# A small GpSimd copy per unit in a fused attention and bilinear kernel

## The chip, the cores and the metric

The kernel runs on one core of one Trainium2 chip. The metric is the device time of one launch in microseconds (us). Times shown for a kernel are the median of its runs.

## The reference

```
scores = (q @ k^T) / 8                           per head; 4 batches, 12 heads, 448 tokens, width 64
scores = einsum('bhij,hg->bgij', scores, w_pre)  mix the heads
attn   = exp(scores - max) / (sum + 1e-9)
attn   = einsum('bhij,hg->bgij', attn, w_post)   mix the heads again
x      = (attn @ v), laid out as 1792 x 768
out    = ((x @ w_a) * (x @ w_b)) @ w_out         768 -> 1536 -> 768
```

## The kernel before

The first 480 us or so are attention, the rest is the bilinear part. The change touches attention alone.

**Units and steps.** The queries of a batch are cut into chunks of 120, 120, 120 and 88 rows, and a chunk into units of 20 (the last of a batch has 8). That makes 16 chunks and 92 units, 23 to a batch. The main loop (L565) runs over steps `s`; step `s` handles unit `s`, and below a step is named by that number, so batch 1 is steps 23 to 45.

**What a step does, in program order.** It gathers the scores of unit `s + 3` (L584), mixes the heads of unit `s` with `w_pre` (`premix`, L590), copies out the second mix of unit `s - 2`, takes maximum and exponential of unit `s` (`smax`, L596), runs the step's share of the products q by k for a later chunk (`qk`) and of attention by v (`av`), turns the row sums of unit `s` into scaled mixing weights `kr` (`norm`, L601), and mixes unit `s - 1` with `w_post` (`postmix`, L604). At the end stand the loads and copies listed in `after` for the step (L605).

**The scores' way.** `qk` writes two heads of a chunk to PSUM; ScalarE copies them to the chunk's tile `s` (L219). There are two such tiles, so chunk `c` writes where chunk `c - 2` stood. A gather is a DMA from SBUF to SBUF on SyncE's queue (SP), four for a unit of 20 rows (L235): it brings the 12 heads of 5 rows onto 60 partitions. So the first copy L219 of a chunk waits until the last gather of the chunk two before has landed. The 88-row chunk of a batch begins its `qk` at the tenth step of the batch (9, 32, 55, 78), and the last unit that reads the tile it overwrites is gathered one step before. The first chunk of the next batch begins at steps 15, 38 and 61, with two heads' products in that step.

**What GpSimd (POOL) issues, in one queue.** `load_v` (L183) loads a sixth of the next batch's v in each of steps 9 to 14 of a batch (batch 0's own v in steps 2 and 4). `load_k` (L187) stands three steps ahead of the `qk` that uses it, which comes to steps 12, 12, 13, 14, 15 and 16 of a batch; `load_q` (L194) four steps ahead, twice a chunk; `spread_q` (L203, L208) is a GpSimd copy that reorders q, one step ahead. The order of the queue is the program's order, but nothing ties it to the step: an entry starts when the one before has been issued and its own buffer is free and data there. Buffers: 10 for k, 3 for raw q, 4 for q, 2 for each half of v.

**Row sums.** `smax` has ScalarE write the row sums `rs` of a block of 10 rows (L265); `norm` has VectorE add 1e-9 to them in place (L272), take the reciprocal (L274) and scale `kf` by it to `kr` (L276). A unit has two blocks; `rs` has 4 buffers.

Of the kernel before, what the change touches and what calls it, by code (L numbers as in the profile page):

```python
# [7 lines left out]
F32 = mybir.dt.float32  # L8
# [13 lines left out]
def talking_heads_bilinear_kernel(  # L22
# [11 lines left out]
    nc = tc.nc  # L34
# [15 lines left out]
    AH = 3  # L50
# [25 lines left out]
    units = []  # L76
# [3 lines left out]
    NU = len(units)  # L80
# [9 lines left out]
    const = ctx.enter_context(tc.tile_pool(name="const", bufs=1))  # L90
# [3 lines left out]
    w_p = ctx.enter_context(tc.tile_pool(name="w", bufs=2))  # L94
# [16 lines left out]

    def ps_t():
        return ps.tile([128, 2, 512], F32, tag="t", name="pst", bufs=1)[:, 0]

    todo_at, now = {}, [0]

# [104 lines left out]
    def halves(n):  # L221
        return [(o, min(QH, n - o)) for o in range(0, n, QH)]

    def gather(u):
        c, o, n = units[u]
        sbt[u] = [sb_p.tile([128, S], F32, tag=f"sb{e}", name="sb") for e in range(2)]
        for i, (t, m) in enumerate(halves(n)):
            r = 64 * (i // 2)
            nb = chunks[c][2] // QB
            k_ = (o + t) // QB  # L230
            if k_ < nb:
                rows = st[c][:nb * QB].rearrange("(i k) h s -> k i h s", k=nb)[k_, t % QB:t % QB + m]
            else:
                rows = st[c][o + t:o + t + m]
            nc.sync.dma_start(out=sbt[u][i % 2][r:r + m * H], in_=rows)  # L235
# [21 lines left out]
    def smax(k_):  # L257
        u, j, n = k_
        m = rows_of(n)
        mp = mt.pop((u, j))  # L260
        nm = w_p.tile([128, 1], F32, tag="nm", name="nm", bufs=4)
        rs = w_p.tile([128, 1], F32, tag="rs", name="rs", bufs=4)
        a = w_p.tile([128, S], F32, tag="an", name="a", bufs=AB)
        nc.vector.tensor_reduce(nm[:m], mp[:m], axis=AXX, op=ALU.max, negate=True)  # L264
        nc.scalar.activation(a[:m], mp[:m], ACTF.Exp, bias=nm[:m], scale=1.0, accum_out=rs[:m])  # L265
        at[u, j] = (a, rs)

    def norm(k_):
        u, j, n = k_
        m = rows_of(n)  # L270
        a, rs = at.pop((u, j))
        nc.vector.tensor_scalar(rs[:m], rs[:m], 1e-9, None, op0=ALU.add)  # L272
        rc = w_p.tile([128, 1], F32, tag="rc", name="rc", bufs=4)
        nc.vector.reciprocal(rc[:m], rs[:m])  # L274
        kr = w_p.tile([128, H, QB], F32, tag="kr", name="kr", bufs=5)
        nc.vector.tensor_scalar(kr[:m], kf[:m], rc[:m], None, op0=ALU.mult)  # L276
        ant[u, j] = a, kr
# [45 lines left out]
    items, after, ready = {}, {}, {}  # L323
# [31 lines left out]
    def load_x(b, parts=(0, 1, 2)):  # L355
        if b not in xt:
            xt[b] = big.tile([128, 2, KD, S], F32R, tag="s" if b < 2 else "pt", name="xhl")
        for i in parts:
            nc.sync.dma_start(out=xt[b].bitcast(F32)[:, 1, 2 * i:2 * i + 2], in_=xd[b][:, 2 * i:2 * i + 2])
# [176 lines left out]
    with tc.manual_schedule():  # L536
        setup()
        load_q(0, 0)
        load_k(0, 0)
        load_k(0, 1)  # L540
        load_q(0, 1)
        load_k(0, 2)
        load_k(0, 3)
        act_table()
        warm_up(WARM)
        setup_mask()
        spread_q(0, 0, nc.vector)
        for i in range(G):
            if i == 1:
                spread_q(0, 1, nc.vector)  # L550
            if i + 4 < G:
                load_k(0, i + 4)
            if i == 2:
                load_q(1, 0)
                load_q(1, 1)
            qk(0, i)
        spread_q(1, 0)
        setup_w()
        nxt_g = AH + 1
        for u in range(nxt_g):  # L560
            gather(u)
        warm_up(WARM3)
        tail = iter(())

        for s in range(NU + 2):  # L565
            now[0] = s
            if s == last_prep + 1:
                open_moe()
                load_raw(order[0])
                later(lambda: load_raw(order[1]), 1)  # L570
                for i in range(3):
                    later(lambda i=i: load_x(0, (i,)), 2 + i)
                tail = tail_ops()
            if s == NU - 2:
                load_x(1)
            if s == NU - 1:
                load_x(2)
            if s in (2, 4):
                for i in range(3):
                    load_v(0, 3 * (s // 2 - 1) + i)  # L580
            b, i = divmod(s, NUB)
            if b + 1 < B and 0 <= i - V_AT < 6:
                load_v(b + 1, i - V_AT)
            while nxt_g <= min(s + AH, NU - 1) and ready.get(units[nxt_g][0], -1) < s:  # L584
                gather(nxt_g)
                nxt_g += 1
            for fn in todo_at.pop(s, ()):
                fn()
            if s < NU:
                premix(s)  # L590
            if s >= 2:
                for k_ in blocks_of(s - 2):
                    evac_p(k_)
            if s < NU:
                for k_ in blocks_of(s):
                    smax(k_)  # L596
            for it in items.get(s, ()):
                it[0](*it[1:])
            if s < NU:
                for k_ in blocks_of(s):  # L600
                    norm(k_)  # L601
            if 0 <= s - 1 < NU:
                for k_ in blocks_of(s - 1):
                    postmix(k_)  # L604
            for it in after.get(s, ()):  # L605
                it[0](*it[1:])
            if s >= last_prep + 2:
                take(tail, RATE if s < NU - LATE else RATE2)
            if s == NU:
                for _ in tail:  # L610
                    pass
                tail = split_ops(1)
                for k_ in blocks_of(NU - 1):
                    evac_p(k_)
                run_a(0, 0)
            if s == NU + 1:
                run_b(0, 0)
        for p in range(6):
            av(NA - 1, p)
        for t in sorted(todo_at):  # L620
            for fn in todo_at[t]:
                fn()
        todo_at.clear()
        load_x(3)
        for _ in tail:
            pass
        now[0] = 999
        late = conv_ops(range(2, 4))
        take(late, T1)
        run_a(0, 1)  # L630
        take(split_ops(2), 12)
        run_b(0, 1)
        take(late, T2)
        run_a(0, 2)
        take(late, T3)
        run_b(0, 2)
        for _ in late:
            pass
        run_a(1, 0)
        take(split_ops(3), 12)  # L640
        run_b(1, 0)
        todo = {(0, 3): order[4], (1, 1): order[5], (1, 2): order[6], (1, 3): order[7]}
        for i, u in enumerate(order[8:]):
            todo[2 + i // 3, i % 3 if u[0] == "f" else 2] = u
        nxt = 6
        pairs = [(0, 3), (1, 1), (1, 2), (1, 3)] + [(f, b) for f in range(2, KF) for b in range(B)]
        for i, (f, b) in enumerate(pairs):
            now[0] = 1000 + i
            for fn in todo_at.pop(now[0], ()):
                fn()  # L650
            if (f, b) in todo:
                ops, fin = conv(todo[f, b])
                for fn in ops:
                    fn()
                if nxt < len(order):
                    load_raw(order[nxt])
                    nxt += 1
            run_a(f, b)
            if (f, b) in todo:
                fin()  # L660
            run_b(f, b)
            if f == KF - 1 and b == 1:
                load_o(0)
                load_h(0)
                load_o(1)
                split_o(0)
            if f == KF - 1 and b > 1:
                for i in range(KF // 2 * (b - 2), KF // 2 * (b - 1)):
                    split_h(0, i)
            if b == B - 1:  # L670
                del wt["f", f]
        now[0] += 1
        for t in sorted(todo_at):
            for fn in todo_at[t]:
                fn()
        todo_at.clear()
        for j in range(B * KD):
            b, m = divmod(j, KD)
            load_o(j + 2)
            if m == 0 and b + 1 < B:  # L680
                load_h(b + 1)
            if j + 1 < B * KD:
                split_o(j + 1)
            if b + 1 < B and m >= 2:
                for f in range(3 * (m - 2), 3 * (m - 1)):
                    split_h(b + 1, f)
            run_o(j)
# [48 lines left out]
```

## Time and profile before

| | us |
|---|---|
| median of 3 runs | 1020.28 |
| the three runs | 1009.82, 1020.28, 1021.34 |
| the profiled execution | 1023.44 |
| its span, first to last instruction | 1021.7 |
| TensorE busy in the span | 977.9 |

Engines are named PE (TensorE matmul), DVE (VectorE), ACT (ScalarE), POOL (GpSimd) and SP (SyncE). A row of a timeline gives start, length, engine, line, operation, what it writes and reads, how many such instructions in a row, and in brackets how long the engine was idle before and what ended that. A row of stretches gives from and to, the length, then busy us and number of instructions of PE, PEld (weight loads), DVE, ACT and POOL, then the mean granted TensorE clock as a share of the full one, the mean busy share of the DMA engines, and GB/s. A row of the waits gives who waited for whom, the total in us, how often and the longest.

### The profile page before, as it was taken

The numbers are of one execution on the slowest core, as the hardware profiler recorded it, in microseconds if no ns is written. First come the engines' busy times: TensorE is split into PE (matmuls) and PEld (weight loads), VectorE is DVE, ScalarE is ACT, GpSimd is POOL, SyncE is SP. The second block draws the span as 40 slices with busy tenths as digits, with TensorE's granted clock in tenths as the row PEclk, the third lists the DMA queues.
The fourth block names the chain that finished last, engine by engine and source line by source line (L and its number), as shares of the span: only waits on it lengthen the run. The fifth ranks groups of instructions, "written<-read, shape, count | busy, mean of one in ns | idle before, by whom it ended". The sixth has DMA issues, their size and how long they took to land.

```text
span 1021.7 us, 16847 instructions
## 1 busy us (share of the span) xinstructions
PE 977.9 (96%) x6388; PEld 777.9 (76%) x6388; DVE 504.8 (49%) x1090; ACT 418.6 (41%) x854; POOL 275.2 (27%) x229
## 2 busy tenths in 40 slices
PE   7799999899999999988999999999999999999998
PEld 4356566556656566666889999999999998999997
DVE  1355445344554445567667565666555364341500
ACT  2576667466656667655321111111111143443421
POOL 4301103110121100002134323332323234554642
PEclk7999999899998999998999999999999999999999
DMA  6544336433354233347335333433323166556431
GB/s 171 158 149 149 99 121 175 151 109 108 123 173 143 87 126 108 107 153 254 111 99 190 133 115 136 144 116 118 142 108 144 74 244 235 208 181 229 157 122 67
DMA packets 63471, 146.59 MB, mean 143 GB/s; under 512 B 6252, under 2 KB 48000, under 8 KB 62368
## 3 DMA queue, kind: packets, MB, share of 16 engines
q1 hardware_dynamic: 58528, 131.11, 37.3%
q0 software_dynamic: 4864, 14.42, 5.1%
q8 instruction: 51, 0.84, 0.3%
q14 instruction: 28, 0.23, 0.1%
HBM read 80.23 MB, written 26.74 MB: 105 GB/s over the span
## 4 chain that ended last, share of the span: by engine, by line
PE 83%; DMA 9%; DVE 3%; ACT 2%; SPq 1%; issue 1%; POOL 0%; ACTq 0%; DVEq 0%
PE pp L286 13%; PE pst L218 8%; PE mp L255 7%; PE xp L311 7%; PE po L435 6%; PE po L436 6%; PE po L434 6%; DMA sb<-s 6%; PE pa L434 5%; PE pa L436 5%; PE pa L435 5%; PE pb L436 5%; PE pb L435 5%; PE pb L434 5%; DMA xd<-xs 3%; ACT s L219 1%
## 5 line engine op out<-in xcount | busy, mean ns | idle before, releaser
L286 PEld LDWEIGHTS pp<-kr,a 124*112 124x112 f32 (+1 forms) x1440 | 161.8, 184 | 51.2 <-issue 31.6
L264 DVE TENSOR_REDUCE nm<-mp 124x1 f32<-124x448 f32 x180 | 104.6, 620 | 160.8 <-PE mp L255 160.8
L286 PE MATMUL pp<-kr,a 124*112 124x120 f32 (+1 forms) x1440 | 179.3, 280 | 3.4 <-ACT pt L297 2.2
L265 ACT ACTIVATE a<-mp,nm 124x448 f32<-124x448 f32 x180 | 112.7, 631 | 94.7 <-DVE nm L264 91.9
L396 POOL TENSOR_TENSOR cvm<-cvm,cvr 128x768 int32<-128x768 int32 x36 | 67.0, 1862 | 281.2 <-DVE cvm L395 211.3
L218 PE MATMUL pst<-k,q 64*120 64x448 f32 (+1 forms) x384 | 102.9, 614 | 25.9 <-ACT s L219 25.8
L424 POOL TENSOR_TENSOR wl<-rawo,wh 128x768 fp32r<-128x768 f32 x48 | 93.7, 1974 | 105.3 <-ACT wh L423 105.3
L297 ACT COPY pt<-pp 112x480 f32<-112x480 f32 x180 | 97.0, 573 | 50.6 <-PE pp L286 50.3
L446 ACT COPY sa<-pa 128x448 f32<-128x448 f32 x48 | 25.6, 534 | 221.8 <-PE pa L436 213.7
L435 PE MATMUL po<-hl,wh 128*128 128x448 f32 x288 | 106.3, 369 | 0.7 <-DVE hl L471 0.7
L435 PE MATMUL pa<-xhl,wh 128*128 128x448 f32 x288 | 104.6, 363 | 1.7 <-DVE xhl L366 1.7
L434 PE MATMUL po<-hh,wh 128*128 128x448 f32 x288 | 106.2, 369 | 0.0
L436 PE MATMUL po<-hh,wl 128*128 128x448 f32 x288 | 106.2, 369 | 0.0
L255 PE MATMUL mp<-sb,wp 60*64 60x448 f32 x720 | 99.3, 567 | 6.7 <-ACT a L265 4.0
L434 PE MATMUL pa<-xhl,wh 128*128 128x448 f32 x288 | 104.6, 363 | 0.0
L436 PE MATMUL pa<-xhl,wl 128*128 128x448 f32 x288 | 104.4, 363 | 0.0
L219 ACT COPY s<-pst 120x896 f32<-120x896 f32 (+1 forms) x96 | 86.5, 901 | 40.2 <-PE pst L218 21.0
L436 PE MATMUL pb<-xhl,wl 128*128 128x448 f32 x282 | 102.3, 363 | 0.6 <-POOL wl L424 0.6
L434 PE MATMUL pb<-xhl,wh 128*128 128x448 f32 x282 | 102.2, 362 | 0.0
L435 PE MATMUL pb<-xhl,wh 128*128 128x448 f32 x282 | 102.2, 362 | 0.0
L218 PEld LDWEIGHTS pst<-k,q 64*120 64x120 f32 (+1 forms) x384 | 27.6, 179 | 95.7 <-ACT s L219 38.6
L471 DVE TENSOR_TENSOR hl<-hl,hh 128x448 fp32r<-128x448 f32 x48 | 57.9, 1261 | 79.4 <-ACT hh L470 79.4
(63 smaller groups left out, 1307.2 us busy)
## 6 DMA issues: line engine op xcount, KB each, us to landing
sb<-s SPq DMA_DIRECT2D x356, 105.0 KB
raw<-in_w_ab_dram SPq DMA_DIRECT2D x24, 768.0 KB
rawo<-wod SPq DMA_DIRECT2D x24, 768.0 KB
hd<-hf SPq DMA_DIRECT2D x48, 224.0 KB
raw<-in_w_out_dram SPq DMA_DIRECT2D x12, 768.0 KB
v<-in_v_dram POOLq DMA_DIRECT2D x24, 224.0 KB, 5.5
xhl<-xd SPq DMA_DIRECT2D x12, 448.0 KB
hl<-hd SPq DMA_DIRECT2D x4, 1344.0 KB
```

Source lines behind the costliest of these rows:

```text
L218: nc.tensor.matmul(sp[:n, g], lhsT=qt[c, i // QG][rows, i % QG], rhs=kt[b, i][rows])
L219: nc.scalar.copy(st[c].rearrange("p (g i) s -> p i g s", g=2)[:n, i], sp[:n])
L255: nc.tensor.matmul(mt[u, i // 2][col:col + M], lhsT=wp[r:r + m, :M], rhs=tiles[i % 2][r:r + m])
L264: nc.vector.tensor_reduce(nm[:m], mp[:m], axis=AXX, op=ALU.max, negate=True)
L265: nc.scalar.activation(a[:m], mp[:m], ACTF.Exp, bias=nm[:m], scale=1.0, accum_out=rs[:m])
L286: nc.tensor.matmul(pp[:, r, :, :n], lhsT=an[:m, r * P:(r + 1) * P], rhs=kr[:m, :, :n])
L297: nc.scalar.copy(ptt[a][:P, :, :, o:o + n], pps.pop((u, j))[:, :, :, :n])
L311: nc.tensor.matmul(xp[64 * e:64 * e + 64, p % 3, :n], lhsT=vt[b, g][:, h % 6, r], rhs=ptt[a][:P, r, h, :n], start=(r == 0), stop=(r == R - 1),
L424: nc.gpsimd.tensor_tensor(ll[:, sl], raw, hh.bitcast(F32)[:, sl], op=ALU.subtract)
L434: nc.tensor.matmul(o, lhsT=hh[:, k0 + kk], rhs=mh[:, kk], start=(kk == 0), stop=False)
L435: nc.tensor.matmul(o, lhsT=hh[:, k0 + kk], rhs=ml[:, kk], start=False, stop=False)
L436: nc.tensor.matmul(o, lhsT=ll[:, k0 + kk], rhs=mh[:, kk], start=False, stop=(kk == n - 1))
```

## The change

Once in each step, GpSimd copies a column of row sums of the unit before into a small tile that nothing reads. Its place in the program is ahead of the step's `load_v`, and the gathers move from behind `load_v` to ahead of that copy. The source is the row-sum tile of the unit's first block after 1e-9 has been added. `rs` gets 24 buffers instead of 4.

```
+    tick = const.tile([128, 1], F32, name="tick")
+    seen = {}
+
+    def pace(u):
+
+        if u in seen:
+            nc.gpsimd.tensor_copy(tick[:60], seen.pop(u)[:60, :1])
...
-        rs = w_p.tile([128, 1], F32, tag="rs", name="rs", bufs=4)
+        rs = w_p.tile([128, 1], F32, tag="rs", name="rs", bufs=24)
...
         nc.vector.tensor_scalar(rs[:m], rs[:m], 1e-9, None, op0=ALU.add)
+        if j == 0 and m > 64:
+            seen[u] = rs
...
+            while nxt_g <= min(s + AH, NU - 1) and ready.get(units[nxt_g][0], -1) < s:
+                gather(nxt_g)
+                nxt_g += 1
+            pace(s - 1)
             if s in (2, 4):
                 for i in range(3):
                     load_v(0, 3 * (s // 2 - 1) + i)
             b, i = divmod(s, NUB)
             if b + 1 < B and 0 <= i - V_AT < 6:
                 load_v(b + 1, i - V_AT)
-            while nxt_g <= min(s + AH, NU - 1) and ready.get(units[nxt_g][0], -1) < s:
-                gather(nxt_g)
-                nxt_g += 1
```

## Rows read from the trace of the kernel before

**Rows 1.** The page, part 1: busy us, share of span, instructions
```profile
PE 977.9 (96%) x6388; PEld 777.9 (76%) x6388; DVE 504.8 (49%) x1090; ACT 418.6 (41%) x854; POOL 275.2 (27%) x229
```
**Rows 2.** Stretches: steps 9-10, 32-33, 55-56 and 78-79
```profile
71.38:82.59 11.21, 9.71 (x89) 6.40 (x88) 4.78 (x15) 6.23 (x15) 2.51 (x5) 1.00 0.45 148
179.70:197.52 17.82, 13.12 (x89) 8.25 (x88) 5.58 (x17) 7.04 (x16) 2.91 (x5) 0.81 0.44 146
296.26:313.70 17.44, 13.05 (x89) 8.25 (x88) 5.58 (x17) 7.04 (x16) 2.90 (x5) 0.80 0.44 144
412.44:422.07 9.63, 9.63 (x89) 6.39 (x88) 4.58 (x17) 6.29 (x15) 0.00 (x0) 1.00 0.27 99
```
**Rows 3.** Stretches: steps 6 and 8
```profile
58.15:64.02 5.87, 5.18 (x29) 2.59 (x29) 2.53 (x9) 3.85 (x9) 0.00 (x0) 1.00 0.33 120
67.70:71.38 3.68, 3.68 (x29) 2.20 (x28) 2.30 (x9) 3.06 (x8) 0.00 (x0) 1.00 0.34 125
```
**Rows 4.** The chain that ended last, around steps 30 to 33: start, us, what
```profile
168.57 13.94 DMA xd<-xs
...
182.53 8.70 DMA sb<-s
...
191.37 0.91 ACT s L219
```
**Rows 5.** Waits of ScalarE
```profile
ACT s L219 <- DMA sb<-s: 19.2, 3, 7.7
```
**Rows 6.** Waits of GpSimd
```profile
POOL q L203 <- PE pst L218: 200.4, 20, 14.3
...
POOL k L187 <- PE pst L218: 64.4, 6, 16.3
POOL v L183 <- PE xp L311: 47.6, 4, 16.6
```
**Rows 7.** Timeline of GpSimd around steps 26 to 30
```profile
157.08 1.65 POOL L183 DMA_DIRECT2D v<-in_v_dram  x3 [16.65 <-PE xp L311]
...
167.21 0.54 POOL L183 DMA_DIRECT2D v<-in_v_dram  x1 [7.18 <-PE xp L311]
...
170.99 0.55 POOL L187 DMA_DIRECT2D k<-in_k_dram  x1
171.53 0.84 POOL L203 COPY q<-qraw 128x360 f32<-128x360 f32 x1
```
**Rows 8.** Timeline of SP's queue: three stretches of gathers
```profile
169.69 32.00 SPq L235 DMA_DIRECT2D sb<-s  x24
...
204.54 6.79 SPq L235 DMA_DIRECT2D sb<-s  x8
...
402.43 23.81 SPq L235 DMA_DIRECT2D sb<-s  x24
```
**Rows 9.** Timeline of VectorE, steps 30 and 31
```profile
171.60 0.86 DVE L276 TENSOR_SCALAR kr<-kf,rc 124x120 f32<-124x120 f32 x1
...
175.29 0.28 DVE L276 TENSOR_SCALAR kr<-kf,rc 124x120 f32<-124x120 f32 x1
...
178.58 0.15 DVE L272 TENSOR_SCALAR rs<-rs 124x1 f32<-124x1 f32 x1 [0.32 <-ACT a L265]
```
**Rows 10.** Timeline of TensorE, steps 31 and 38
```profile
176.02 0.98 PE L255 MATMUL mp<-sb,wp 60*64 60x448 f32 x8
...
177.88 1.90 PE L286 MATMUL pp<-kr,a 124*112 124x120 f32 x16
...
217.71 1.02 PE L218 MATMUL pst<-k,q 64*120 64x448 f32 x4
```
**Rows 11.** GpSimd's groups by line, its smallest copy: busy us, mean ns
```profile
L208 POOL COPY q<-qraw 128x24 f32<-128x24 f32 x8 | 1.6, 205 | 0.0
```
**Rows 12.** DMA issues: how many, KB each, median us to landing
```profile
k<-in_k_dram POOLq DMA_DIRECT2D x18, 224.0 KB, 9.4
...
qraw<-in_q_dram POOLq DMA_DIRECT2D x20, 180.0 KB, 5.7
```

## The prediction

> **What bounds the kernel now.** I read the page first, then the timelines of TensorE, GpSimd and SP's queue against each other, then the chain of waits and stretches cut at the starts of steps. The page says that TensorE is busy 977.9 of 1021.7 us [rows 1], so no edit to another engine is worth more than some 44 us of idle time plus what a low clock costs. GpSimd is busy for 27% and bounds nothing; what it can do to the end lies in when its loads start.
>
> The step to look at is the tenth of each batch. The same two steps, with the same 89 matmuls, take 9.63 us in batch 3, but 17.82 us in batch 1, 17.44 us in batch 2 and 11.21 us in batch 0 [rows 2]. In batch 3 TensorE is busy throughout at a full granted clock. [...] The chain shows what it waits for: a gather (sb<-s) lands 8.70 us after the link before it, and only then does ScalarE copy the first scores of the 88-row chunk (L219) into the tile that this gather was still reading [rows 4]. ScalarE has three such waits, 19.2 us in all, the longest 7.7 us [rows 5], and by the stretches they fall in batches 0, 1 and 2.
>
> Batch 3 has the same gathers and the same stores of x, but no loads for a next batch. What differs is GpSimd's queue. Its waits [rows 6] are for TensorE to give back buffers of q (200.4 us in 20 waits), of k and of v: it has run ahead of the program's step until no buffer was free. Ahead of step 32 it waits 16.65 us for v's buffer with everything queued behind, issues three loads of v at 157.08 us, waits 7.18 us again, and from 167.21 to 171.5 us issues eight loads in a row, of 224 KB each but one [rows 7], some 1.75 MB. By the program the three belong to steps 32 to 34 and the eight to steps 35 to 37, all after 179.70 us; they come six to eight steps early and land on the gathers of steps 29 to 31. SP's queue shows the price: 24 gathers in a row take 32.00 us there, and 23.81 us in batch 3 [rows 8]. The 8.2 us between them are about 1 us a load.
>
> **The change part by part.** The copy `pace(s - 1)` waits for VectorE's add in `norm` of unit `s - 1`. That add comes at 178.58 us in step 31, which began at 176.02 us [rows 9, 10]: 2.6 us into the step. So what GpSimd has to do in step `s` is issued no earlier than 2.6 us into step `s - 1`, one step early at most, where before it was up to eight early.
>
> *The stall goes.* The batch's fourteen loads of v, k and q for the next one are then spread over steps 32 to 39, one to three a step, all behind the gather that the copy L219 in step 32 waits for. Only a load of q for step 31 still stands beside that gather. Taking batch 3 as the undisturbed price, the three stretches give 17.82 - 9.63 = 8.19, 17.44 - 9.63 = 7.81 and 11.21 - 9.63 = 1.58 us, 17.6 us together [rows 2]. Step 6 of batch 0 may give 2.2 more: it has 29 matmuls in 5.87 us, where step 8 has as many in 3.68 us [rows 3]; but batch 0's own v now comes in steps 2 and 4, and three of these loads stand ahead of step 6. I take 0 of it and keep 2.2 as an end.
>
> *The copies themselves.* There are 92, one a unit. No row shows a 60x1 copy; the nearest is GpSimd's 128x24 copy at 205 ns [rows 11]. Between 0 and 205 ns each they are 0 to 19 us of an engine that is idle for most of attention. I take 205 ns, and nothing on the path. VectorE signals one engine more and ScalarE may check one buffer more per unit; with VectorE busy 4.58 and ScalarE 6.29 of 9.63 us in the undisturbed stretch [rows 2] I take 0 for both. The trace shows neither; if each unit paid a tenth of a smallest copy, 0.02 us, it would be 1.9 us.
>
> *What is queued behind the wait.* Loads and q's reordering copies, and later the weight conversion. A reordering copy stands one step ahead of its product; now it starts at the earliest 2.6 + 0.2 us into the step before its own and lasts 0.84 us [rows 7], so it ends 3.7 us into that step. The product comes about 1 us into the step after its own, at least two steps of 3.68 us later [rows 3]: 4.7 us of margin. A load of q has three steps before that copy, 11 us against a landing of 5.7; a load of k has four steps from issue to use, in steps 11 to 14 about 19 us, less 4 us for its place in the queue, against 9.4 [rows 12]. None is late. The conversion begins after step 83, and its GpSimd part waits for VectorE work that comes behind the same `norm` anyway: 0. The waits for TensorE's buffers [rows 6] disappear into the new wait; both are idle time of an idle engine: 0.
>
> *The moved gathers.* They are SP's alone. They pass `load_v`, which is POOL's, and no other entry of SP's queue; SP's order is what it was: 0. The 24 buffers of row sums let GpSimd lag twelve units behind, which it never does: 0.
>
> *The new collision with VectorE.* A reordering copy now follows the pace copy at once, just when VectorE computes `kr`. The one `kr` at 171.60 us that met such a copy (171.53 us) took 0.86 us instead of 0.28 [rows 7, 9]. Of the 30 copies 28 stand behind a pace copy, so this may happen 28 times, at 0.58 us or some more. It is hidden: the first `kr` of step 30 is there at 175.57 us and the mix that needs it, in step 31, starts at 177.88 us [rows 9, 10], 2.3 us later. Without that cover it would be 16 us.
>
> [...]
>
> The sum, against the profiled execution: 1023.44 - 17.6 = 1005.8 us, 1.72% less. That execution lies 0.3% above the median of the runs shown; the same share of 1020.28 gives 1002.7 us. Beyond it lie the 2.2 us of step 6 and whatever a higher clock after steps 38 and 61 gives; short of it lie the 1.9 us of signals and what the loads do in their new place.
>
> **The rivals.** *The loads find the next boundary.* Steps 9 to 14 of a batch now hold 12 loads, at 1 us each. They must be through before the copy L219 of step 15, which overwrites the tile that the gather of step 14 reads. Before, that gather had been issued by 211.3 us and the copy could start at 218.7 us [rows 8, 10], 7.4 us later. Six steps of 4.8 us against four gathers of some 0.85 us each (8 in 6.79 us [rows 8]) leave 1.4 us a step (4.8 is half of the 9.63 us), 8.4 us; the other 3.6 us eat into the 7.4. So it decides at about 16 us of load work, a third more than I reckon. Then steps 15, 38 and 61 stall: 1.5 us each, as in batch 0, takes 4.7 us of the gain and gives about 1007; 8.2 us each, as in batch 1, is 24.6 us, more than the gain, and gives 1027 us, slower than before. For it speaks that backlog drains slowly: the gather that ends the stall began to be waited for at 182.53 us, 11 us after the burst [rows 4, 7]; against it the mean DMA share of 0.44 to 0.45 [rows 2].
>
> *The loads are not the cause.* The chain passes through a store of x, xd<-xs, for 13.94 us [rows 4]. If it is that store in SP's queue that holds the gathers up, pacing GpSimd moves nothing, and the time stays at 1020. Against it: batch 3 has that store in the same place and no stall.
>
> [...]
>
> **How the numbers follow.** The stalls go and nothing takes their place: 0.63, at 1002.7, with a range of its own of 996 to 1008. A small stall comes back, about 1007 to 1015: 0.18. Loads not the cause, or lock not hidden, 1019 to 1020: 0.13. A full stall at the next boundary, 1027: 0.06. The range from 996 to 1016 takes in the first two. Faster by more than 2%, which is about what a measurement of this kernel can tell from no change, means below 999.9 us: the first case with step 6 and a better clock, 0.28. Slower by over 2% needs more than 1040.7 us, stalls at several boundaries: 0.03. The rest, 0.69, is within 2%; my time itself lies there.
>
> **What would show it.** GpSimd's waits should name VectorE's `rs`, and the waits for pst and xp should be gone. Its loads should stand singly, in the steps of the program, none between steps 26 and 31. Steps 32 and 33, and 55 and 56, should take about 9.6 us at a clock of 1.00, and ScalarE's wait for sb<-s should vanish. Stretched `kr` should be more than the few of before, with no wait of the mix for `kr`. I am wrong if the two steps still take 17 us, or if TensorE's waits for the copy L219 grow at steps 15, 38 and 61.

## The result, and the profile after

Over 20 runs each, the changed kernel has a median of 1010.62 us and the kernel before 1022.85 us. The ratio is 0.991, with a 95% interval of 0.9889 to 0.9932: 0.9% faster, less than the 2% that counts as a difference here, inside the range, and about half of the 1.72% that was forecast. The ratio is that of the means of the fast runs, 1010.67 and 1019.81 us, and leaves out the runs over 1.5% above the fastest of their kernel: seven of the 20 before and one after. The changed kernel's profiled execution has a span of 1008.6 us against 1021.7 us.

The stretches of the steps forecast to change, in the changed kernel: steps 9-10, 32-33 and 55-56, then steps 15, 38 and 61. Columns as in [rows 2].

```profile
65.17:75.64 10.47, 9.71 (x89) 6.40 (x89) 4.90 (x17) 6.22 (x15) 1.65 (x5) 1.00 0.44 146
182.18:191.82 9.64, 9.64 (x91) 6.40 (x90) 4.66 (x17) 6.31 (x15) 1.57 (x5) 1.00 0.41 132
294.94:304.58 9.64, 9.64 (x91) 6.40 (x90) 4.66 (x17) 6.30 (x15) 1.57 (x5) 1.00 0.42 134
94.91:110.87 15.96, 7.18 (x33) 4.22 (x32) 2.64 (x9) 4.93 (x10) 2.35 (x5) 0.70 0.47 155
211.08:223.75 12.67, 7.18 (x34) 4.22 (x33) 2.66 (x9) 4.94 (x10) 2.37 (x5) 0.74 0.47 158
323.84:336.49 12.65, 7.18 (x34) 4.22 (x33) 2.65 (x9) 4.93 (x10) 2.36 (x5) 0.74 0.45 155
```

The first three answer to [rows 2]: the stall for which these steps took 17.8 and 17.4 us is gone in batches 1 and 2, to within 0.01 us of batch 3's 9.63; batch 0 keeps 0.8 us of its 1.6. The other three are the next boundary. The kernel before took this there:

```profile
101.86:108.63 6.77, 4.71 (x34) 2.49 (x33) 2.50 (x9) 4.81 (x10) 0.00 (x0) 1.00 0.38 125
216.79:225.18 8.39, 6.33 (x33) 3.87 (x32) 2.50 (x9) 4.81 (x10) 0.00 (x0) 0.80 0.32 104
332.98:341.37 8.39, 6.33 (x34) 3.75 (x33) 2.50 (x9) 4.79 (x10) 0.00 (x0) 0.80 0.32 102
```

Steps 9-10, 32-33 and 55-56 fell from 46.5 to 29.8 us, 16.7 us less. Steps 15, 38 and 61 rose from 23.6 to 41.3 us, 17.7 us more. The gain was paid back in full six steps later. The mean granted clock in those steps was 0.70 and 0.74, where it had been 1.00 and 0.80.

The waits of GpSimd in the changed kernel, which answer to [rows 6] (waited for: us in total, times, longest us); [rows 5] are answered by the row after them:

```profile
POOL tick L121 <- DVE rs L280: 344.9, 88, 13.8
...
POOL v L191 <- issue: 6.1, 20, 0.4
```

And those of ScalarE for gathers, in the same kernel:

```profile
ACT s L227 <- DMA sb<-s: 16.8, 4, 6.6
```

The change does what it says: one wait for the row sums has replaced the waits for TensorE's buffers. But ScalarE still waits 16.8 us for gathers, where it waited 19.2 us; 13.2 of them now lie in steps 15, 38 and 61 (6.6, 3.3 and 3.3 us).

The timeline of GpSimd around steps 12 and 13 shows the loads at their new place, one to three behind each pace copy:

```profile
79.67 0.18 POOL L121 COPY tick<-rs 60x1 f32<-60x1 f32 x1 [2.66 <-DVE rs L280]
80.14 0.55 POOL L191 DMA_DIRECT2D v<-in_v_dram  x1 [0.29 <-issue]
80.68 1.10 POOL L195 DMA_DIRECT2D k<-in_k_dram  x2
...
84.97 0.54 POOL L191 DMA_DIRECT2D v<-in_v_dram  x1 [0.30 <-issue]
85.51 0.56 POOL L202 DMA_DIRECT2D qraw<-in_q_dram  x1
86.06 0.55 POOL L195 DMA_DIRECT2D k<-in_k_dram  x1
```

And the chain that ended last shows what they do there. In this trace and in that of the kernel before, SP's queue never had more than eight transfers under way: no gather was issued before the transfer eight ahead of it had landed, and 45 of the changed kernel's 360 went within 0.1 us of that landing.

```profile
71.81 8.43 DMA sb<-s
...
80.30 13.35 DMA sb<-s
...
94.44 10.00 DMA sb<-s
...
104.67 0.92 ACT s L227
```

The gather issued at 80.30 us landed at 93.65 us, and the next one went at 93.66 us; the last of step 14, issued right behind that at 94.44 us, landed at 104.44 us, and only then could ScalarE's copy begin that step 15 waited for.

The rest of the 13.1 us between the two spans, and so all of what is left of the gain, lies where the forecast looked little or not at all: step 3 begins 4.0 us earlier (43.08 in place of 47.10 us), step 6 lost its 2.2 us, steps 87 to 90 are 2.5 us shorter, and the 864 products of the last part take 6 to 7 ns less each, 5.4 us of busy time in sum:

```profile
L445 PE MATMUL po<-hl,wh 128*128 128x448 f32 x288 | 104.5, 363 | 0.7 <-DVE hl L481 0.7
L444 PE MATMUL po<-hh,wh 128*128 128x448 f32 x288 | 104.4, 362 | 0.0
```

In the kernel before the same group stood at 369 ns:

```profile
L434 PE MATMUL po<-hh,wh 128*128 128x448 f32 x288 | 106.2, 369 | 0.0
```

### The profile page after: what moved, and what is told of

Same layout as the page of the kernel before. It is cut to its first block, busy times and chain, and to the rows that moved or that the text cites. A ratio compares the mean times of both kernels' runs of the same rounds, so it can differ in the third digit from the quotient of the medians.

```text
span 1008.6 us, 17007 instructions
## 1 busy us (share of the span) xinstructions
PE 962.7 (95%) x6388; PEld 774.4 (77%) x6388; DVE 513.1 (51%) x1090; ACT 418.5 (41%) x854; POOL 293.0 (29%) x321
## 4 chain that ended last, share of the span: by engine, by line
PE 82%; DMA 11%; DVE 3%; ACT 2%; SPq 1%; issue 1%; POOL 0%; ACTq 0%; DVEq 0%
PE pp L296 13%; DMA sb<-s 10%; PE pst L226 7%; PE mp L263 7%; PE xp L321 6%; PE po L445 6%; PE po L446 6%; PE po L444 6%; PE pa L444 5%; PE pa L445 5%; PE pa L446 5%; PE pb L446 5%; PE pb L444 5%; PE pb L445 5%; ACT s L227 1%; DVE xhl L376 1%
## 5 line engine op out<-in xcount | busy, mean ns | idle before, releaser
L296 PEld LDWEIGHTS pp<-kr,a 124*112 124x112 f32 (+1 forms) x1440 | 159.7, 182 | 50.7 <-issue 33.0
L226 PE MATMUL pst<-k,q 64*120 64x448 f32 (+1 forms) x384 | 100.1, 599 | 30.9 <-ACT s L227 30.8
L121 POOL COPY tick<-rs 60x1 f32<-60x1 f32 x92 | 17.1, 186 | 344.9 <-DVE rs L280 344.9
L263 PE MATMUL mp<-sb,wp 60*64 60x448 f32 x720 | 95.2, 564 | 3.8 <-ACT a L273 3.5
```

The source lines that it names most:

```text
L226: nc.tensor.matmul(sp[:n, g], lhsT=qt[c, i // QG][rows, i % QG], rhs=kt[b, i][rows])
L263: nc.tensor.matmul(mt[u, i // 2][col:col + M], lhsT=wp[r:r + m, :M], rhs=tiles[i % 2][r:r + m])
L296: nc.tensor.matmul(pp[:, r, :, :n], lhsT=an[:m, r * P:(r + 1) * P], rhs=kr[:m, :, :n])
```

## The experiments

Ratios are to the kernel before, run on the same chip. Where no ratio is given there is one time, taken beside the trace.

### Which loads make the new stall

The changed kernel with the loads of v seven steps later:

```
-    V_AT = 9
+    V_AT = 16
```

> The changed kernel, with the six loads of v in steps 16 to 21 of a batch in place of 9 to 14, so that only six of the twelve loads stand ahead of the gather that step 15 waits for. Theory A (the loads' work ahead of that gather makes the new stall): steps 15, 38 and 61 fall from 15.96, 12.66 and 12.64 us to between 6.7 and 8.4 us, as before the change; steps 32 and 33 stay at 9.6 us; 17 us less than the changed kernel, about 994 us, ratio to the kernel before 0.972 to 0.98. Theory B (the loads of k, three steps ahead of their use and issued by the paced queue, make the stall): steps 15, 38 and 61 stay above 12 us and the time at about 1010 us.

Measured: 994.67 us, ratio 0.9769 (0.9686 to 0.9853). Its steps 9-10, 32-33, 15, 38 and 61:

```profile
65.18:74.81 9.63, 9.63 (x89) 6.39 (x88) 4.58 (x17) 6.21 (x15) 0.68 (x3) 1.00 0.33 120
171.94:181.58 9.64, 9.64 (x90) 6.40 (x89) 4.58 (x17) 6.29 (x15) 0.68 (x3) 1.00 0.27 99
...
94.08:100.87 6.79, 4.71 (x34) 2.49 (x33) 2.62 (x9) 4.82 (x10) 2.88 (x6) 1.00 0.62 180
200.85:207.63 6.78, 4.70 (x33) 2.48 (x32) 2.62 (x9) 4.82 (x10) 2.87 (x6) 1.00 0.53 153
307.61:315.90 8.29, 6.21 (x34) 3.89 (x33) 2.62 (x9) 4.81 (x10) 2.87 (x6) 0.81 0.52 155
```

Both stalls are gone in this trace, and 19.4 us with the second. ScalarE waits for a gather one single time, for 2.5 us. What is left in step 15, 2.1 us of TensorE's idle time (6.79 less 4.71 us), is the pair of products that share one PSUM buffer, as before the change, where TensorE waited 2.1 us there for ScalarE's copy out of that buffer. The loads of k stood where they stood, so they alone do not make the stall. A second run gave the same:

> The changed kernel with v in steps 16 to 21, unchanged from the earlier run, for a tighter interval and in one session with the two runs on the address. Theory A: 990 to 998 us, ratio to the kernel before 0.97 to 0.98, steps 15, 38 and 61 at 6.7 to 8.4 us. Theory B (the first time was luck): above 1000 us.

Measured: 993.61 us, ratio 0.9746 (0.9671 to 0.9821). Steps 15, 38 and 61 took 8.02, 6.79 and 8.13 us, but steps 9 and 10 of batch 0 took 10.90 us, where the first trace had 9.63: in batch 0 the old boundary is not always cleared. The eight runs of this version (989.71 to 997.92 us) all lie below the fastest run of either kernel. Both intervals lie below 1; that the gain is more than 2% they do not show.

To see whether all loads since step 9 count or only the last ones, v was moved by three steps alone (`V_AT = 12`):

> The changed kernel with the loads of v in steps 12 to 17 in place of 9 to 14: nine loads in place of twelve in steps 9 to 14, and the same eight as before in steps 12 to 14. Theory A (all loads since step 9 pile up in front of the gather of step 14): steps 38 and 61 between the two ends measured, 12.65 us with twelve loads and 6.8 to 8.4 with six, about 10 us. Theory B (only the loads of steps 12 to 14 count, what came in steps 9 to 11 has drained): 12.6 us or more, as with all twelve.

Measured: 1006.83 us. Steps 15, 38 and 61:

```profile
98.60:111.47 12.87, 7.19 (x34) 4.22 (x33) 2.62 (x9) 4.93 (x10) 3.43 (x7) 0.77 0.52 174
211.88:220.92 9.04, 5.99 (x34) 3.68 (x33) 2.56 (x9) 4.94 (x10) 3.51 (x7) 0.85 0.64 192
321.22:331.12 9.90, 6.32 (x33) 3.93 (x32) 2.57 (x9) 4.93 (x10) 3.52 (x7) 0.83 0.61 186
```

Steps 38 and 61 lie between the two ends, with the same loads in steps 12 to 14 as in the changed kernel. So the loads of steps 9 to 11 count too: the work piles up over six steps. Step 15 of batch 0 came out above 12.6 us, at 12.87, but below the changed kernel's 15.96.

### The pace without the later place, and the place without the pace

The kernel before with the loads of v at the later steps and no pace (the same edit to `V_AT`, in the kernel before):

> The kernel before, without any copy, with the loads of v in steps 16 to 21 of a batch in place of 9 to 14. Theory A (a load's place in time counts, and without the pace GpSimd still runs ahead): the loads of v come when the loads of k ahead of them have got their buffers, around steps 10 and 11, behind the gather of step 8; steps 32 and 33 lose part of their stall, steps 15, 38 and 61 gain one; about 1005 to 1015 us. Theory B (only the pace removes the stall): steps 32 and 33 stay at 17 us or more, about 1020 us.

Measured: 1018.12 us, ratio 0.9958 (0.9914 to 1.0001), just above the band of theory A. Its second trace:

> The kernel before with v in steps 16 to 21 and no copy, for a second trace of it. Theory A (the burst now follows the release of the buffers of k, after step 9): steps 32 and 33 at 9.6 us together, steps 38 and 61 at 12.7 to 13.1 us as in the first trace. Theory B (the first trace was chance): steps 32 and 33 at 16 us or more, or steps 38 and 61 at 8.4 us.

Measured: 1026.64 us; steps 32-33, 15 and 38 of that trace (step 61 took 12.32 us):

```profile
180.34:189.98 9.64, 9.64 (x89) 6.40 (x89) 4.68 (x15) 6.30 (x15) 3.09 (x6) 1.00 0.46 147
...
96.01:109.27 13.26, 6.43 (x33) 3.57 (x32) 2.50 (x9) 4.91 (x10) 0.00 (x0) 0.74 0.41 141
209.25:221.82 12.57, 6.52 (x33) 3.66 (x33) 2.50 (x9) 4.91 (x10) 0.00 (x0) 0.73 0.42 143
```

Without any pace the move of v alone clears steps 32 and 33, and makes the very stall at step 15 that the pace alone made; the first trace had 12.87, 13.13 and 12.74 us there. The stall's length hangs on where the loads land, whoever puts them there. Only pace and place together clear both boundaries. The time of this version understates what the place does to attention: in both of its traces all groups of products of the bilinear part stood at 369 ns, and the kernel before has six of its nine large ones at 362 to 363 (the last products, below).

The copy for unit 0 alone, with all else of the change in place:

```
-        if u in seen:
+        if u == 0 and u in seen:
```

> As the changed kernel (gathers ahead of the loads of v, 24 buffers of row sums, the small tile), but the copy runs for unit 0 alone, so GpSimd is free to run ahead from step 1 on. Theory A (the pace alone moves the time; moved gathers and buffers are nothing): steps 32 and 33 together take about 17.8 us as before, the whole about 1020 us, ratio 0.995 to 1.005. Theory B (part of the gain lies in where the new buffers put the other tiles): the products of the last part (L444 to L446, po) start 200 ns apart as in the changed kernel's profile and not 207 ns as before, worth 864 x 7 ns = 5.9 us, so about 1014 us.

Measured: 1025.04 us, ratio 1.0056 (1.0014 to 1.0098). Steps 32-33 and 55-56 stall as before the change:

```profile
188.74:204.82 16.08, 12.04 (x89) 7.85 (x89) 5.35 (x17) 6.94 (x16) 2.91 (x5) 0.91 0.45 149
303.80:321.29 17.49, 13.12 (x90) 8.25 (x89) 5.58 (x17) 7.04 (x16) 2.91 (x5) 0.81 0.45 147
```

Step 4 of batch 0 had a stall of its own in this kernel:

```profile
49.47:65.73 16.26, 5.98 (x29) 3.77 (x28) 2.49 (x9) 4.43 (x9) 2.04 (x4) 0.69 0.47 158
```

The 24 buffers and the moved gathers move neither stall; the copies do. The one copy held batch 0's v back until 26.84 us and then let ten loads of v and four of q go by 44.7 us, ahead of step 4's copy, which waited 10.8 us for a gather. No theory had that; it is the same mechanism at a third boundary, at 12.6 us over the 3.68 us of that step in the changed kernel.

### The first steps

The copy from unit 5 on (`if u >= 5 and u in seen:`):

> The changed kernel, but with the copy only from unit 5 on, so that GpSimd runs ahead in the first steps as before. Theory A (the 4 us that the profile shows gained by step 3 come from the loads of batch 0's v no longer standing in front of the first gathers): the first mix begins at 25.3 us as before and not at 21.7 us, and the time is 3 to 6 us above the changed kernel, about 1015 us. Theory B (that gain is chance of the one profile): the first mix at about 21.7 us and about 1010.6 us.

Measured: 1007.94 us, ratio 0.9881 (0.9813 to 0.9949). The first mix began at 23.28 us, between the two theories, and step 3 at 42.63 us, earlier than in the changed kernel, with batch 0's v issued at 12.2 and 15.2 us as in the kernel before. So the pace of the first steps is not where the 4 us come from. A second trace of the changed kernel was taken for this and for the last products:

> The changed kernel, unchanged, for a second trace. Theory A (what its profile showed is its own): steps 15, 38 and 61 at 12 to 16 us, steps 32 and 33 at 9.6 us, last products at 362 ns, about 1010 us; step 3 begins at 43 us again. Theory B for the start and the last products (chance): step 3 begins at 45 us or later, or the last products at 369 ns.

Measured: 1011.24 us, step 3 at 44.71 us, steps 15, 38 and 61 at 11.82, 12.38 and 12.30 us, the last products at 362 to 363 ns. The stalls at the new boundary came again, and so did the last products; of the 4 us at the start 1.6 did not come again. Steps 9 and 10 of batch 0 took 14.56 us in this trace, where the first had 10.47: in the first batch the old boundary is not safe either, and what the one boundary gained the other lost: the six stretches sum to 70.3 us in this trace and to 71.0 in the first.

### GpSimd's copies beside VectorE's `kr`

Behind each pace copy a second GpSimd copy of 0.83 us, in the version with v at step 16:

```
+            nc.gpsimd.tensor_copy(wide, wide)
```

(`wide` is a 128x360 tile that VectorE zeroes once.)

> The changed kernel with v in steps 16 to 21 (the fastest so far, 994.7 us), and behind each pace copy a second GpSimd copy of 128x360 elements onto itself, about 0.83 us, 92 times in all. It meets VectorE's kr in every unit in place of 28 of 92. Theory A (a kr stretched by GpSimd's copy is hidden behind TensorE, by 2.3 us): some 90 or more of the 180 kr take over 350 ns, none of the mixes waits for kr more than before, and the time is 990 to 998 us. Theory B (it is on the path): 64 more collisions at 0.58 us or more add 37 us or more, 1030 us or above.

Measured: 1005.32 us. Of 180 `kr`, 103 took over 350 ns. The group of `kr` in the kernel before:

```profile
L276 DVE TENSOR_SCALAR kr<-kf,rc 124x120 f32<-124x120 f32 x180 | 54.3, 302 | 6.3
```

In the changed kernel:

```profile
L286 DVE TENSOR_SCALAR kr<-kf,rc 124x120 f32<-124x120 f32 x180 | 63.3, 352 | 6.3
```

With the second copy:

```profile
L289 DVE TENSOR_SCALAR kr<-kf,rc 124x120 f32<-124x120 f32 x180 | 83.9, 466 | 6.3
```

TensorE's only wait for it, with the second copy:

```profile
PE pp L299 <- DVE kr L289: 1.7, 1, 1.7
```

The changed kernel and the version with v at step 16 have one such wait of 1.1 us each. With three times as many collisions, VectorE's time for `kr` rises by 20.6 us and TensorE's wait by 0.6 us: hidden, so theory A holds in its mechanism and B, at 1030 us or above, falls. The time missed A's band by 7.3 us, but not in attention: step 91, the last of the loop, began at 458.5 us here and at 458.6 us in the next run, which has the tile and not the copies. What is missing lies behind it: from the first to the last of the last products 179.1 us in place of 173.5 (groups at 367 to 368 ns), and some 2 us in the products ahead of them. The same tile without the copies was run to see whether the place of the tiles in memory slows the products:

> The changed kernel with v in steps 16 to 21 and the 360-column tile of the wide-copy run, zeroed once but not copied. All tiles stand where they stood in the wide-copy run, whose last products had a mean of 367 ns. Theory A (place): 367 to 369 ns again and some 998 to 1001 us. Theory B (not place, but what GpSimd did or chance): 362 ns and about 993 us.

Measured: 997.68 us, products at 362 to 363 ns. So the place of the tiles alone does not do it.

### The last products

Five more runs were aimed at the 5.4 us in the last part. Their expectations name the time from one start to the next, 200 or 207 ns; the profile's groups give the mean length of one product, 362 or 369 ns. Both tell the same two rates. The kernel before, unchanged:

> The kernel before, unchanged, for a second trace of it. Theory A (of the 13.1 us between the two profiles, 5.6 lie in a part that the change does not touch and belong to that one execution of the kernel before, whose last products start 207 ns apart): this trace shows 200 ns there and a span of about 1014 to 1016 us. Theory B (they belong to the kernel): 207 ns again. Of the start: if step 3 begins at 47 us again, the 4 us that the changed kernel gains there belong to the change; if it begins anywhere between 42 and 47 us, they are chance.

Measured: 1022.07 us; the products at 369 ns again, step 3 at 47.28 us, steps 32-33 and 55-56 at 16.92 and 16.99 us. Theory B. Then the changed kernel's small tile without its copies:

```
+    tick = const.tile([128, 1], F32, name="tick")
...
+        nc.vector.memset(tick, 0.0)
```

> The kernel before with the changed kernel's small tile of one column, which VectorE sets to zero once and nothing else touches. It moves every later tile up by 32 bytes in a partition, the operands of the last products (hl, hh) from an address that is 32 modulo 64 to one that is 0. So far 207 ns between these products was seen in all five traces with hl at 32, and 200 ns in all five with hl at 0. Theory A (the address sets it, and the changed kernel got 5.6 us of its gain from the tile's place and not from the pace): 200 ns, the stalls at steps 32 and 55 as before, about 1014 to 1017 us, and a narrower spread of runs than the kernel before shows. Theory B (the address is nothing): 207 ns, 1020 to 1023 us.

Measured: 1016.40 us, ratio 0.9932 (0.9886 to 0.9978), products at 362 ns, steps 32-33 and 55-56 at 16.92 and 17.35 us, runs from 1010.29 to 1028.81 us, spread as widely as the kernel before. A tile that nothing reads, with no pace and both stalls in place, brings 0.7% by itself. The row sums with 5 buffers instead of 4:

> The kernel before with 5 buffers of row sums in place of 4. It moves the weights (wh, wl) by 32 bytes, to 32 modulo 64 as in the changed kernel, and leaves hl, hh at 32 as before. Theory A (the address of the moving operand hl, hh sets the pace of the last products): 207 ns. Theory B (the address of the weights sets it): 200 ns.

Measured: 1034.10 us, and 368 to 369 ns in all groups of the bilinear part. The changed kernel with the small tile 9 columns wide:

> The changed kernel with the small tile 9 columns wide, of which the copy still writes one: later tiles move by 64 bytes in place of 32, so that hl and hh stand at 32 modulo 64 as in the kernel before, and only the pace is left of the change. Theory A (address): the last products 207 ns apart, the steps as in the changed kernel (9.6 us for steps 32 and 33, 12.6 for step 38), about 5.6 us above the changed kernel, 1014 to 1019 us, with a wider spread of runs. Theory B (the address is nothing): 200 ns and about 1010.6 us.

Measured: 1008.96 us, ratio 0.9887 (0.9822 to 0.9951), steps 15, 38 and 61 at 14.90, 12.22 and 11.96 us, and 362 to 363 ns: theory A of the address falls. The kernel before with that wider tile:

> The kernel before with a tile of 9 columns (64 bytes in place of 32) that VectorE zeroes once. The moving operand of the last products stands at 32 modulo 64, as in the kernel before and in the changed kernel with the wide tile. Theory A (every move of the tiles off the place they had frees the last products): their groups at 362 ns mean as with the 32-byte tile. Theory B (place modulo 64 counts in kernels that do not pace): 369 ns.

Measured: 1019.62 us; the last products at 362 ns, but the ones ahead of them at 367 and 368, which had been at 363 in the kernel before:

```profile
L436 PE MATMUL pa<-xhl,wh 128*128 128x448 f32 x288 | 105.9, 368 | 0.0
...
L436 PE MATMUL po<-hh,wh 128*128 128x448 f32 x288 | 104.3, 362 | 0.0
```

So there are two rates, and which one a group of products gets does not follow the operand's address modulo 64. Of 17 traces 11 had the last products at 362 to 363 ns and six at 367 to 369. Of the nine with the pace one had the longer time (the one with the second copy), of the three with the small tile and at most one copy none, and of the five with neither all. So this gain comes with the small tile even where no pace runs (two traces, one of them with a single copy), and need not be owed to the pace; by what way it comes, and why the second copy lost it, is open. The traces divide cleanly at the start of step 91 (two traces each, one for the idle tile):

| | step 91 begins, us | from there to the end, us |
|---|---|---|
| kernel before | 478.6, 477.2 | 543.1, 543.1 |
| idle tile alone (one column) | 478.5 | 537.5 |
| place alone | 474.7, 471.2 | 553.8, 553.7 |
| pace alone, the changed kernel | 471.2, 472.2 | 537.4, 537.3 |
| pace and place | 450.5, 453.8 | 537.5, 537.5 |

In attention the change gains 5 to 7 us, the place alone 3 to 7, and pace and place together 23 to 28. Behind attention the changed kernel gains 5.7 us, as the idle tile does, and the place alone loses 10.6. In the four kernels that were traced twice the second trace had the rates of the first.

## Why the prediction was wrong in size

**Right: what bounded the kernel, and that this stall goes.** The queue of GpSimd had run ahead, its burst held up the gather before the tenth step, and pacing it removed 16.7 us of the 17.6 us put on it (12.6 in the changed kernel's second trace, where batch 0 stalled for longer); step 6 gave its 2.2 us too, which had been left out. The waits for buffers vanished and the loads stood in their steps, as said. A pace copy took 0.186 us against 0.205 taken from the nearest row, and no wait of TensorE names it. Its group in the changed kernel (busy us, mean ns | idle before, and for what):

```profile
L121 POOL COPY tick<-rs 60x1 f32<-60x1 f32 x92 | 17.1, 186 | 344.9 <-DVE rs L280 344.9
```

**Right: what was costed at nothing.** Moved gathers and 24 buffers clear no stall (the run with one copy). Stretched `kr` rose from 7 of 180 over 350 ns to 31, some at 1.2 us, and TensorE's wait for them stayed at 1.1 us. All 31 stood beside work of GpSimd: 18 met a reordering copy and took 0.36 to 1.27 us, 13 met the issue of a load and took 0.35 to 0.39 us; the 46 `kr` that met nothing of GpSimd's and the 86 that met a pace copy alone took 0.28 to 0.29 us. As forecast, the longer `kr` did not reach the end time. What makes them longer no run shows. The forecast's chance for "lock not hidden" names a lock that no run shows; what the runs showed in its place are these lengths, and a wait of TensorE for `kr` of 1.1 us, or of 1.7 us in the run with 103 longer ones.

**Wrong: "the stalls go and nothing takes their place", at 0.63.** The rival "the loads find the next boundary" came instead, at 0.24 with its two sizes of 1.5 and 8.2 us a step. It came between them: 9.2, 4.3 and 4.3 us, 17.7 us together, against 16.7 us gained. The time of 1010.62 us lies in the band of its small size, 1007 to 1015, but that is luck: by itself the new stall would have left nothing of the gain.

The term that was mis-sized is that rival's margin. It set 7.4 us between the last issue of step 14's gather and the copy it must precede, and let 3.6 us of backlog eat into it. But a gather must land, not only be issued, and the forecast's own [rows 4] had one that took 8.70 us. By the updates of the semaphores in the trace of before, that last gather in batch 1 (step 37) was issued at 210.60 us and landed at 215.92; ScalarE came to the copy at 219.83 us. The margin was 3.9 us. In the changed kernel the same gather was issued at 206.74 us and landed at 217.33, 10.6 us in place of 5.3, and from the first issue of the eight to the last went 7.9 us in place of 6.1. Against the start of its step the landing came 7.1 us later; that ate the 3.9 us and left ScalarE the wait of 3.3 us. SP's queue with these eight gathers, in batch 0 and in batch 1 ([rows 8] have 6.79 us for the latter), and the link of the chain ahead of the copy in batch 1:

```profile
83.64 11.53 SPq L243 DMA_DIRECT2D sb<-s  x8
...
198.83 8.64 SPq L243 DMA_DIRECT2D sb<-s  x8
...
205.36 10.81 DMA sb<-s
...
217.54 0.92 ACT s L227
```

**Wrong: what spoke against it.** The mean DMA share of 0.44 to 0.45 was read as room. In the changed kernel's stalled steps 15, 38 and 61 it stands at 0.45 to 0.47, and in the version without stalls at 0.52 to 0.62. The share is a mean over 16 engines; what was late is the chain of gathers, eight deep, each 7 to 13 us behind the one eight before it. In the traces of the two kernels each of the 356 gathers of 5 rows on SyncE's queue updates its semaphore six times, once about 1.2 us after its issue (the median) and five times more by its landing, and each of the 24 stores of x 16 times. How many engines a gather uses, and which of them the loads use too, no run shows; that sharing them makes the gathers slow is the author's guess, as no run changed the shape of a gather.

**Right in direction, for a part of the time that was not forecast.** The two boundaries cancel to a microsecond. By the two traces the gain comes from step 6, the start, the end of attention and the last products. The start cannot be credited to the pace: step 3 began between 42.6 and 47.6 us in traces of paced kernels and between 44.4 and 48.9 us in the others. The last products gain the same 5.7 us with the idle tile alone, so nearly half of the 13.1 us between the two traces need not be the pace's. So the time fell inside the range by luck, by terms that the prediction did not have.

## What to carry to other kernels

A queue that runs ahead is a matter of where its bursts land: here pacing it moved the load onto the next point of the schedule that had too little slack, where 17.7 us were lost against 16.7 us gained, so price every such point, not only the one that stalls now, and count to the landing of the transfer and not to its issue. Then pick the steps for the loads together with the pace: here the pace alone brought 0.9%, the place alone 0.4% (with an interval that reaches no change), and both together 2.3 to 2.5%. A mean DMA share well below one told nothing of the chain of dependent transfers here: steps stalled at a share of 0.45 to 0.47, and did not at 0.52 to 0.62. And a gain of half a percent can come from the mere presence of a new tile: run the tile without what it is for.

## What the runs showed of the hardware that was not expected

Most groups of the 128x448 products of the bilinear part run at one of two rates, 362 to 363 or 367 to 369 ns mean, at a granted clock of 1.00 in both: the kernel before had groups at both rates with that clock from 484 to 1018 us. The run with the second copy had its three groups of `pa` at 365 ns. Products of one part can differ: in the kernel with the wider idle tile those of `pa` with `wh` had 367 and 368 ns and those with `wl` 363. The operand's address modulo 64 does not decide it: with `hl` and `hh` at 32 the last products took 369 ns in the kernel before and 362 to 363 in the changed kernel with the tile of 9 columns. And the changed kernel repeats itself better: 19 of the changed kernel's 20 runs lie between 1007.25 and 1014.84 us, those of the kernel before between 1009.82 and 1034.87.

The latency of a gather stretched at a DMA share that looked like room. The first one in the chain of the kernel before, ahead of the first mix, took 3.74 us:

```profile
23.14 3.74 DMA sb<-s
```

With up to eight in flight and loads beside them, the links of the changed kernel's chain from 56 to 104 us took 7.02 to 13.35 us, at a mean DMA share of 0.55 over that stretch.
